# A gated long convolution: pitch of the x2 rows, and the order in which the gate copies leave PSUM

## The chip, the cores and the metric

The kernel runs on one core of one Trainium2 chip. The metric is the time of one execution on the device in microseconds; the median of several executions is compared.

## What is computed

Two layers follow each other. The first is a gated linear recurrence over time, the second multiplies three projections of its output, one of which has gone through a circular convolution of the full sequence length (written with Fourier transforms in the reference). There are 4 sequences of 6272 steps with 256 channels.

```
# first layer
f = lower_bound + (1 - lower_bound) * sigmoid(f_logit);  i = 1 - f
for t in range(S):                      # S = 6272
    h = f[:, t] * h + i[:, t] * x[:, t];  y[:, t] = h
# second layer, on y
x1, x2, x3 = split(y @ w_proj, 3)       # 256 channels each
x2_conv = irfft(rfft(x2, axis=1) * rfft(filter_fft, axis=0), axis=1)
out = (x1 * x2_conv * x3) @ w_out
```

## The kernel before

**Stages.** For each sequence b: `hgrn(b)` loads f_logit and x in 13 chunks of 512 steps, takes the sigmoid on ACT (line 303), multiplies on POOL (line 305, tile XT), transposes both on TensorE (line 312) and scans on DVE (line 334); the state is kept transposed in HA, in f16. `spectrum(b)` projects x2 (`phase_p`), makes the first transform step out of it (`phase_f1`, line 655, and `unit`'s line 700), multiplies by the filter's transform (line 713, DVE; line 705 fills one slot of each product on POOL) and transforms back (line 723, copied to Th at line 272). `gate(b)` makes x1 and x3 and their product z. `phase_o(b)` finishes the convolution (line 756), multiplies by z (line 762), projects (line 774), copies (line 274) and stores (line 784).

**Order.** All operations are entered in a plan with their readers and writers, and are then given out in the order that is written out in the string ORDER. It fixes for every operation the engine and the PSUM bank, so every engine has a fixed sequence in which the four sequences' stages are interleaved: hgrn of sequence b+1, spectrum, gate and output of sequence b run side by side. The costs written beside the operations take no part any more when the order is given. The change leaves ORDER as it is. Waits between engines are semaphores derived from the tiles that are read and written.

**The x2 rows.** A sequence of 6272 = 128 x 49 steps is laid out as 49 residues r (Q = 49) on the free side and 128 on the partitions. X2 holds for each of 128 pairs of channels one row of PW = 113 elements in f16: 49 residues of one channel at 0, a gap of 15 zeros at 49 to 63 (eight of them, tile Hm, later hold a part of the filter's transform), and 49 residues of the other channel at 64. `phase_p` fills it: for each group of four residues 8 matmuls (line 642) put 4 x 256 values in PSUM, and one copy (lines 272 and 277, by engine; profile name X<-PS) writes them to X2 as runs of four f16, one run for each channel, 256 runs in all. The thirteenth group has one residue, and writes 256 single elements. `phase_f1` reads 128 elements from the start of each row as the weights of a matmul, 15 elements into the next row when the pitch is 113. In the preparation X2 serves as a landing buffer for the filter (tags raw), and two memsets zero the gaps and the end (lines 571 and 574). The filter itself goes through a tile of the same layout in f32, f2, with the same pitch.

**The gate.** For each of 13 chunks of ten blocks of 49 steps (the last has eight), and each half of the channels, two matmul pairs (line 361) put x1 and x3, 490 values per partition in order of time, in PSUM. ACT copies each to SBUF (line 373, tiles x1s and x3s, f32, two buffers each, in turn), and POOL multiplies them (line 377) into zt, where the residue comes first and the block second: it writes runs of ten f16. Before the change the copies keep the order of time, and the product reads both tiles with steps of 49 elements.

Of the kernel before, what the change touches and what calls it, by code (L numbers as in the profile page):

```python
# [10 lines left out]
F32R = mybir.dt.float32r  # L11
F16 = mybir.dt.float16
I32 = mybir.dt.int32
AOP = mybir.AluOpType
AF = mybir.ActivationFunctionType
# [9 lines left out]
Q = 49  # L25
# [10 lines left out]
NEP = 128  # L36
# [3 lines left out]
HS = 64.0 / S  # L40
ZS = 64.0
OS = 1.0 / 4096.0
PW = 113
NX2 = 13
WR = 3072
AW = 4096
# [142 lines left out]
def kernel(  # L189
# [10 lines left out]
    nc = tc.nc  # L200
# [4 lines left out]
    op = plan.op  # L205

    konst = ctx.enter_context(tc.tile_pool(name="konst", bufs=1))
    iden = konst.tile([128, 128], F32, name="iden")
# [21 lines left out]

    X2 = konst.tile([128, NEP * PW + 16], F16, name="X2")
    xv = X2[:, 0:NEP * PW].rearrange("m (i c) -> m i c", c=PW)

# [10 lines left out]
    late = {}  # L244
# [4 lines left out]
    PS = psp.tile([128, 8, 512], F32, name="PS")  # L249
# [98 lines left out]
    def gate(b):  # L348
        for c in range(NCHK):
            m0 = c * XR  # L350
            nm = min(XR, 128 - m0)
            hn = [("hn", kh, i) for kh in range(2) for i in range(max(c - 1, 0), c + 1)]
            t0, n = m0 * Q, nm * Q
            for jb in range(2):
                x13 = []
                for i in range(2):
                    js = slice(i * 256 + jb * 128, i * 256 + jb * 128 + 128)

                    def mm(e, p, js=js, t0=t0, n=n):
                        for kh in range(2):  # L360
                            nc.tensor.matmul(PS[:, p, 0:n], W13[:, kh, js],  # L361
                                             HA[:, HB[kh] + t0:HB[kh] + t0 + n],
                                             start=(kh == 0), stop=(kh == 1))
                    x13.append(op("x13", {"PE": 0.005 + 2 * n / 2400.0}, mm,
                                  r=hn + ["W13"], w=["qX"], take=1))
                j = count["s"] % 2
                count["s"] += 1

                def xs(i, j=j, n=n):
                    return late["x3s" if i else "x1s"][:, j, 0:n]  # L370
                for i in range(2):
                    op("xs", {"ACT": 0.05 + n / 1200.0}, lambda e, p, xs=xs, n=n, i=i:
                       nc.scalar.activation(  # L373
                           xs(i), PS[:, p, 0:n], AF.Copy, scale=1.0 if i else ZS),
                       r=["cv"], w=[("x1s", j, i)], src=x13[i])
                op("z", {"POOL": 0.1 + 3.68 * n / 1000}, lambda e, xs=xs, jb=jb, m0=m0, nm=nm:
                   nc.gpsimd.tensor_tensor(  # L377
                       late["zt"][:, jb, :, m0:m0 + nm],
                       xs(0).rearrange("p (m r) -> p r m", r=Q),
                       xs(1).rearrange("p (m r) -> p r m", r=Q), op=AOP.mult),  # L380
                   r=[("x1s", j, 0), ("x1s", j, 1), "cv"], w=[("z", jb, c)])


    def prepare(tmp):
        dve, pool, act = nc.vector, nc.gpsimd, nc.scalar
# [13 lines left out]
        for i in range(2):  # L399
            small(lambda e, i=i: dve.tensor_copy(rot[:, i * 128:(i + 1) * 128], iden[:]), 128,  # L400
                  r=["iden"], w=["rot"], kind="turns")
# [16 lines left out]
        for kh in range(2):  # L418
# [4 lines left out]
               r=["om"] + Wr(1), w=["W13"])  # L423
            for p in range(2):
# [4 lines left out]
                   r=["om"] + Wr(1), w=["W2"])  # L429
# [5 lines left out]
        w = scr[:, 2016:4080].bitcast(F32)  # L435
# [24 lines left out]
        def args(e):  # L460
# [42 lines left out]
           w=["v", "sin"], table="sin")  # L503
# [30 lines left out]
        for i in range(WARM):  # L534
            op("warm", {"PE": 0.435}, warm, r=["iden"], take=1)

        f2 = tmp.tile([128, NEP * PW + 16], F32R, name="f2")

        def gaps(e):

            pool.tensor_copy(f2[:, 0:NEP * PW].rearrange("m (i c) -> m i c", c=PW)[:, :, Q:64],
                             iden[:, 0:15].unsqueeze(1).broadcast_to([128, NEP, 15]))
            pool.tensor_copy(f2[:, NEP * PW:], iden[:, 0:16])
        small(gaps, 1920, r=["iden"], w=["f2e"], e="POOL", kind="pad")
        afs = tmp.tile([128, 2, 2, UE, 64], F32R, name="afs")
        fv = f2[:, 0:NEP * PW].rearrange("m (g p c) -> m p g c", p=2, c=PW)
        ff = moe_filter_fft.rearrange("(a r) d -> a r d", r=Q)
        for g, r0 in enumerate(range(0, Q, 4)):
            rn = min(4, Q - r0)
# [21 lines left out]
        op("pad", {"POOL": 2.0}, lambda e: nc.gpsimd.memset(  # L571
            X2[:, 0:NEP * PW].rearrange("m (i c) -> m i c", c=PW)[:, :, Q:64], 0.0),
           w=[("raw", i) for i in range(7)] + [("x2", g) for g in range(NX2)] + ["Hm"])
        op("pad", {"POOL": 0.1}, lambda e: nc.gpsimd.memset(X2[:, NEP * PW:], 0.0),
           w=[("x2", 1)])
        mX = tmp.tile([128, 2, NEP], F32R, name="mX")
        for u in range(NU):
            af = afs[:, u % 2]
            for h in range(2):

                def first(e, pb, j=u * UE + h * 4):
                    pa = PS[:, pb:pb + 2].rearrange("m a (i c) -> m (a i) c", c=256)
                    for i in range(4):
                        nc.tensor.matmul(pa[:, i, :], f2[:, (j + i) * PW:(j + i) * PW + 128],  # L584
                                         D1r[:].rearrange("m x k -> m (x k)"), start=True, stop=True)
                f1 = op("FF1", {"PE": 0.475}, first,
                        r=[("f2", g, p) for g in range(13) for p in range(2)] + ["D1r", "f2e"],
                        w=[("FF1", u, h)], take=2)
                op("afs", either(512), lambda e, pb, af=af, h=h: copy(
                    e, af[:, :, 4 * h:4 * h + 4],  # L590
                    PS[:, pb:pb + 2].rearrange("p a (i x r k) -> p r (a i) x k", x=2, r=2, k=64)
                    [:, :, :, 0]), w=[("af", u % 2, h)], src=f1)
            small(lambda e, af=af, u=u: pool.tensor_copy(
                mX[:, :, u * UE:(u + 1) * UE], af[:, :, :, 0]), 100,
                r=[("af", u % 2, 0), ("af", u % 2, 1)],
                w=["mX"], e="POOL", kind="mX")

            def second(e, pb, af=af):
                for r in range(2):
                    for e2 in range(2):  # L600
                        rows = slice(64 * e2, 64 * e2 + 64)
                        nc.tensor.matmul(PS[:TB, pb + e2, :], FTr[rows, r, 0:TB], af[rows, r],  # L602
                                         start=(r == 0), stop=(r == 1))
            f2nd = op("FF2", {"PE": 0.45}, second,
                      r=[("af", u % 2, 0), ("af", u % 2, 1), "FTr"], w=[("FF2", u)], take=2)
            hw, ht = hws[u % len(hws)][0], [hws[u % len(hws)][1]]
            op("hw", either(1024), lambda e, pb, hw=hw: copy(e, hw[:TB], PS[:TB, pb:pb + 2], HS),
               w=ht, src=f2nd)
            for i, (p0, n) in enumerate(((0, TB), (TB, 64))):
                op("hst", {"SP": 0.36}, lambda e, hw=hw, u=u, p0=p0, n=n: nc.sync.dma_start(  # L610
                    H[u][p0:p0 + n], hw[0:n].rearrange("p e k -> p (e k)")),
                   r=ht, w=[("H", u, i)], dma=0.6 - 0.25 * i, lag=1.7)
# [233 lines left out]
```

## Time and profile before

| what | value |
|---|---|
| median of 3 runs | 494.39 us (493.84 to 494.9) |
| profiled execution | 494.1 us |
| its span, from the first to the last instruction | 492.3 us |
| granted TensorE clock | 0.998 |
| products of x1 and x3 on POOL (line 377) | 104, 201.5 us busy |
| copies of x1 and of x3 on ACT (line 373) | 208, 122.2 us busy |
| copies of x2 on DVE, on ACT (X<-PS) | 29 and 23, 41.6 and 33.9 us busy |
| POOL, busy in the span | 74% |

The profile is one execution, taken by the hardware profiler. A group of instructions is named by its source line, its engine, its operation, and its output and inputs; busy time is summed, and a mean duration of one is given in nanoseconds. Idle time of an engine is put down to whoever ended it. The chain is followed back from the last instruction, at each step to what released it. TensorE's matmuls overlap each other, so its busy time is not a measure of its use. Tile names are shortened where they end in digits: X is X2, f is f2, D is D1; HA also holds the first transform's output A.

### The profile page before, as it was taken

The numbers are of one execution on the slowest core, as the hardware profiler recorded it, in microseconds if no ns is written. First come the engines' busy times: TensorE is split into PE (matmuls) and PEld (weight loads), VectorE is DVE, ScalarE is ACT, GpSimd is POOL, SyncE is SP. The second block draws the span as 40 slices with busy tenths as digits, with TensorE's granted clock in tenths as the row PEclk, the third lists the DMA queues.
The fourth block names the chain that finished last, engine by engine and source line by source line (L and its number), as shares of the span: only waits on it lengthen the run. The fifth ranks groups of instructions, "written<-read, shape, count | busy, mean of one in ns | idle before, by whom it ended". The sixth has DMA issues, their size and how long they took to land.

```text
span 492.3 us, 13180 instructions
## 1 busy us (share of the span) xinstructions
PE 474.2 (96%) x5257; PEld 373.5 (76%) x5257; DVE 430.6 (87%) x449; ACT 427.7 (87%) x618; POOL 364.9 (74%) x299
## 2 busy tenths in 40 slices
PE   7999999999999999999999999999989999999894
PEld 6888788767768999677677888667778897666683
DVE  7678998799999998889989989899989988898773
ACT  5988899899999879899899888999888878999554
POOL 5587767899999425999999536999898443999700
PEclk9999999999999999999999999999999999999999
DMA  8979989575696899286857996467867861444166
GB/s 333 397 275 309 322 293 327 158 230 172 198 271 199 276 357 293 68 257 205 259 158 270 348 312 185 150 203 234 267 236 266 342 223 53 143 140 156 46 262 263
DMA packets 41725, 116.39 MB, mean 236 GB/s; under 512 B 4384, under 2 KB 6304, under 8 KB 41664
## 3 DMA queue, kind: packets, MB, share of 16 engines
q1 hardware_dynamic: 41664, 115.56, 69.9%
q8 instruction: 41, 0.67, 0.6%
q14 instruction: 20, 0.16, 0.1%
HBM read 84.54 MB, written 31.00 MB: 235 GB/s over the span
## 4 chain that ended last, share of the span: by engine, by line
PE 75%; ACT 7%; POOL 6%; DMA 5%; issue 3%; DVE 3%; SPq 0%; ACTq 0%; DVEq 0%; POOLq 0%
PE PS L312 15%; PE PS L361 13%; PE PS L642 9%; PE PS L774 8%; PE PS L723 7%; PE PS L700 5%; PE PS L655 5%; PE PS L756 5%; PE PS L584 3%; POOL zt L377 3%; DMA out_dram<-osb 2%; DVE PP L713 2%; PE PS L602 2%; ACT osb L274 2%; DMA FL<-in_f_logit_dram 2%
## 5 line engine op out<-in xcount | busy, mean ns | idle before, releaser
L377 POOL TENSOR_TENSOR zt<-x1s,x3s 128x490 f16<-128x490 f32 (+1 forms) x104 | 201.5, 1959 | 23.7 <-ACT x3s L373 16.2
L305 POOL TENSOR_TENSOR XT<-XT,FL 128x1024 f32<-128x1024 f32 (+1 forms) x52 | 117.3, 2258 | 58.7 <-ACT FL L303 41.1
L713 DVE TENSOR_TENSOR PP<-PS,Hu 98x1008 f16<-98x1008 f32 x128 | 147.4, 1199 | 11.3 <-ACT x3s L373 4.6
L334 DVE TENSOR_TENSOR_SCAN HA<-fTs,HA,PS 128x512 f16<-128x512 f32 (+1 forms) x96 | 113.9, 1203 | 5.2 <-PE PS L312 2.8
L361 PE MATMUL PS<-HA,W 128*128 128x490 f16 (+1 forms) x416 | 106.7, 368 | 1.4 <-ACT x3s L373 0.6
L762 DVE TENSOR_TENSOR ys<-PS,zt 128x1024 fp32r<-128x1024 f32 (+1 forms) x52 | 59.3, 1150 | 12.1 <-PE PS L756 7.3
L326 ACT ACTIVATE fTs<-PS,nomc 128x512 f32<-128x512 f32 (+1 forms) x87 | 59.2, 682 | 10.4 <-PE PS L312 8.3
L274 ACT ACTIVATE osb<-PS 128x1024 f32<-128x1024 f32 (+1 forms) x51 | 50.2, 990 | 19.7 <-PE PS L774 15.3
L373 ACT ACTIVATE x1s<-PS 128x490 f32<-128x490 f32 (+1 forms) x104 | 61.4, 594 | 5.5 <-PE PS L361 3.2
L373 ACT ACTIVATE x3s<-PS 128x490 f32<-128x490 f32 (+1 forms) x104 | 60.8, 590 | 5.5 <-PE PS L361 3.6
L312 PE MATMUL PS<-iden,XT 128*128 128x128 f32 x392 | 61.9, 278 | 0.7 <-POOL XT L305 0.3
L312 PE MATMUL PS<-iden,FL 128*128 128x128 f32 x392 | 61.0, 276 | 0.7 <-DVE X L277 0.7
L774 PE MATMUL PS<-Wo,ys 128*128 128x256 f32 x392 | 58.6, 293 | 1.0 <-DVE ys L762 0.8
L723 PEld LDWEIGHTS <-PP 98*128 98x128 f16 x1024 | 49.9, 98 | 11.9 <-issue 3.5
L272 ACT CAST Th<-PS 128x784 f16<-128x784 f32 x64 | 53.5, 836 | 2.6 <-PE PS L723 2.0
L303 ACT ACTIVATE FL<-FL 128x1024 f32<-128x1024 f32 (+1 forms) x52 | 53.0, 1022 | 1.5 <-DMA FL<-in_f_logit_dram 1.5
L361 PEld LDWEIGHTS <-W 128*128 128x128 f16 x416 | 35.1, 98 | 25.1 <-issue 7.4
L723 PE MATMUL PS<-VA,PP 98*128 98x98 f16 x512 | 52.2, 207 | 1.6 <-DVE PP L713 1.3
L774 PEld LDWEIGHTS PS<-Wo,ys 128*128 128x128 f32 x392 | 49.6, 189 | 4.8 <-DVE ys L762 1.8
L312 PEld LDWEIGHTS PS<-iden,XT 128*128 128x128 f32 x392 | 44.4, 140 | 10.9 <-issue 3.0
L723 PE MATMUL PS<-VB,PP 98*128 98x98 f16 x512 | 52.0, 207 | 0.0
L272 ACT CAST HA<-PS 128x1024 f16<-128x1024 f32 x49 | 50.3, 1032 | 1.6 <-PE PS L655 1.0
(105 smaller groups left out, 697.8 us busy)
## 6 DMA issues: line engine op xcount, KB each, us to landing
Hu<-H SPq DMA_DIRECT2D x64, 392.0 KB
FL<-in_f_logit_dram SPq DMA_DIRECT2D x48, 512.0 KB
XT<-in_x_dram SPq DMA_DIRECT2D x48, 512.0 KB
out_dram<-osb SPq DMA_DIRECT2D x48, 512.0 KB
X<-in_moe_filter_fft_dram SPq DMA_DIRECT2D x9, 512.0 KB
H<-Hu SPq DMA_DIRECT2D x16, 196.0 KB
H<-Hu SPq DMA_DIRECT2D x16, 128.0 KB
Hu<-in_moe_filter_fft_dram SPq DMA_DIRECT2D x2, 512.0 KB
```

What stands on the lines that cost most here:

```text
L272: nc.scalar.copy(dst, src)
L274: nc.scalar.activation(dst, src, AF.Copy, scale=scale)
L305: op("u", {"POOL": 0.1 + 0.553 * nb}, lambda e, xt=xt, ft=ft: nc.gpsimd.tensor_tensor(xt, xt, ft, op=AOP.mult), r=[("ft", k)], w=[("xt", k)])
L312: nc.tensor.transpose(PS[:, p, j:128 * nb:nb], src[:, j, cols], iden[:])
L334: nc.vector.tensor_tensor_scan(h, fT, PS[:, p, 0:n], init, op0=AOP.mult, op1=AOP.add),
L361: nc.tensor.matmul(PS[:, p, 0:n], W13[:, kh, js], HA[:, HB[kh] + t0:HB[kh] + t0 + n], start=(kh == 0), stop=(kh == 1))
L373: nc.scalar.activation(xs(i), PS[:, p, 0:n], AF.Copy, scale=1.0 if i else ZS),
L377: nc.gpsimd.tensor_tensor(late["zt"][:, jb, :, m0:m0 + nm], xs(0).rearrange("p (m r) -> p r m", r=Q), xs(1).rearrange("p (m r) -> p r m", ...
L713: nc.vector.tensor_tensor(PP[:TB, k, o, :, :, 1:64], px.unsqueeze(1).broadcast_to([TB, 2, UE, 63]), hh[:, :, :, 1:64], op=AOP.mult)
L723: nc.tensor.matmul(PS[:, ib + o, pr * TB:(pr + 1) * TB], PP[:TB, k, o, n, 2 * pr:2 * pr + 2, :], v[:TB], start=(n == 0), stop=(n == 1))
L762: nc.vector.tensor_tensor(late["ys"][:, yk, :, 0:rn * 128], PS[:, cb:cb + 2, 0:rn * 128], late["zt"][:].rearrange("p k r m -> p k (r m)") ...
L774: nc.tensor.matmul(po[:, i, :], late["ys"][:, yk, kh, i * 128:(i + 1) * 128], Wo[:, kh, :], start=(kh == 0), stop=(kh == 1))
```

## The change

The pitch of X2 becomes 116, while f2 keeps 113 under a name of its own (PF). The three elements at the end of each row, which the matmul weights of line 655 now read too, are zeroed by one more memset in the preparation. In the gate the copies on ACT read PSUM with the residue first and the block second, in steps of 49 elements, and write one run; the product then reads both tiles in one run. Its output, the number of instructions apart from the memset, and the order are the same.

```diff
-PW = 113
+PW = 116
+PF = 113
...
                 def xs(i, j=j, n=n):
-                    return late["x3s" if i else "x1s"][:, j, 0:n]
+                    return late["x3s" if i else "x1s"][:, j, 0:n].rearrange("p (r m) -> p r m", r=Q)
                 for i in range(2):
                     op("xs", {"ACT": 0.05 + n / 1200.0}, lambda e, p, xs=xs, n=n, i=i:
                        nc.scalar.activation(
-                           xs(i), PS[:, p, 0:n], AF.Copy, scale=1.0 if i else ZS),
+                           xs(i), PS[:, p, 0:n].rearrange("p (m r) -> p r m", r=Q), AF.Copy,
+                           scale=1.0 if i else ZS),
                        r=["cv"], w=[("x1s", j, i)], src=x13[i])
                 op("z", {"POOL": 0.1 + 3.68 * n / 1000}, lambda e, xs=xs, jb=jb, m0=m0, nm=nm:
                    nc.gpsimd.tensor_tensor(
                        late["zt"][:, jb, :, m0:m0 + nm],
-                       xs(0).rearrange("p (m r) -> p r m", r=Q),
-                       xs(1).rearrange("p (m r) -> p r m", r=Q), op=AOP.mult),
+                       xs(0), xs(1), op=AOP.mult),
...
-        f2 = tmp.tile([128, NEP * PW + 16], F32R, name="f2")
+        f2 = tmp.tile([128, NEP * PF + 16], F32R, name="f2")
...
-        op("pad", {"POOL": 0.1}, lambda e: nc.gpsimd.memset(X2[:, NEP * PW:], 0.0),
-           w=[("x2", 1)])
+
+        def tails(e):
+            nc.gpsimd.memset(xv[:, :, 113:PW], 0.0)
+            nc.gpsimd.memset(X2[:, NEP * PW:], 0.0)
+        op("pad", {"POOL": 0.6}, tails, w=[("raw", i) for i in range(7)] + [("x2", 1)])
...
-                        nc.tensor.matmul(pa[:, i, :], f2[:, (j + i) * PW:(j + i) * PW + 128],
+                        nc.tensor.matmul(pa[:, i, :], f2[:, (j + i) * PF:(j + i) * PF + 128],
```

More of the change, by code (lines that the diff above doesn't have):

```diff
@@ L535, in prepare @@
             op("warm", {"PE": 0.435}, warm, r=["iden"], take=1)
-        f2 = tmp.tile([128, NEP * PW + 16], F32R, name="f2")
+        f2 = tmp.tile([128, NEP * PF + 16], F32R, name="f2")
         def gaps(e):
-            pool.tensor_copy(f2[:, 0:NEP * PW].rearrange("m (i c) -> m i c", c=PW)[:, :, Q:64],
+            pool.tensor_copy(f2[:, 0:NEP * PF].rearrange("m (i c) -> m i c", c=PF)[:, :, Q:64],
                              iden[:, 0:15].unsqueeze(1).broadcast_to([128, NEP, 15]))
-            pool.tensor_copy(f2[:, NEP * PW:], iden[:, 0:16])
+            pool.tensor_copy(f2[:, NEP * PF:], iden[:, 0:16])
         small(gaps, 1920, r=["iden"], w=["f2e"], e="POOL", kind="pad")
         afs = tmp.tile([128, 2, 2, UE, 64], F32R, name="afs")
-        fv = f2[:, 0:NEP * PW].rearrange("m (g p c) -> m p g c", p=2, c=PW)
+        fv = f2[:, 0:NEP * PF].rearrange("m (g p c) -> m p g c", p=2, c=PF)
         ff = moe_filter_fft.rearrange("(a r) d -> a r d", r=Q)
```

## The prediction

> **What bounds the kernel now.** I read the page's busy times first, then the chain that ended last.
>
> ```profile
> span 492.3 us, 13180 instructions
> ...
> PE 474.2 (96%) x5257; PEld 373.5 (76%) x5257; DVE 430.6 (87%) x449; ACT 427.7 (87%) x618; POOL 364.9 (74%) x299
> ...
> PE 75%; ACT 7%; POOL 6%; DMA 5%; issue 3%; DVE 3%; SPq 0%; ACTq 0%; DVEq 0%; POOLq 0%
> PE PS L312 15%; PE PS L361 13%; PE PS L642 9%; PE PS L774 8%; PE PS L723 7%; PE PS L700 5%; PE PS L655 5%; PE PS L756 5%; PE PS L584 3%; POOL zt L377 3%; DMA out_dram<-osb 2%; DVE PP L713 2%; PE PS L602 2%; ACT osb L274 2%; DMA FL<-in_f_logit_dram 2%
> ```
>
> TensorE is the frame: three quarters of the chain are its matmuls. POOL holds 6% of the chain, half of it the products of line 377, which the change shortens. I therefore asked next how long anybody stands still for POOL, or for the x2 copies (tile X), in the waits:
>
> ```profile
> POOL zt L377 <- ACT x3s L373: 16.2, 13, 9.0
> ...
> PEld L723 <- POOL PP L705: 2.6, 6, 1.0
> ...
> ACT x3s L373 <- POOL zt L377: 1.2, 3, 0.6
> ...
> PEld PS L312 <- DVE X L277: 1.1, 1, 1.1
> ...
> PEld PS L312 <- POOL XT L305: 0.9, 3, 0.5
> ...
> PEld L655 <- DVE X L277: 0.7, 2, 0.4
> ...
> PE PS L642 <- ACT X L272: 0.6, 1, 0.6
> ```
>
> (Total us, times, longest.) The waits are short. POOL, in turn, waits 16.2 us for the copies that feed it. Last I read single costs, with shapes kept apart:
>
> ```profile
> L377 POOL TENSOR_TENSOR zt<-x1s,x3s 128x490 f16<-128x490 f32 x96 | 188.7, 1986 | 23.0 <-ACT x3s L373 15.5 <-DVE ys L762 6.2 <-ACT x1s L373 0.6
> ...
> L305 POOL TENSOR_TENSOR XT<-XT,FL 128x1024 f32<-128x1024 f32 x48 | 114.4, 2385 | 47.3 <-ACT FL L303 36.6 <-DMA XT<-in_x_dram 7.6 <-PE PS L312 1.9
> ...
> L373 ACT ACTIVATE x3s<-PS 128x490 f32<-128x490 f32 x96 | 56.6, 595 | 4.7 <-PE PS L361 2.8 <-POOL zt L377 1.2 <-ACT x1s L373 0.2
> L272 ACT CAST Th<-PS 128x784 f16<-128x784 f32 x64 | 53.5, 836 | 2.6 <-PE PS L723 2.0
> ...
> L274 ACT ACTIVATE osb<-PS 128x1024 f32<-128x1024 f32 x48 | 49.0, 1027 | 19.5 <-PE PS L774 15.3 <-PE PS L756 2.2 <-DMA out_dram<-osb 1.4
> ...
> L277 DVE CAST X<-PS 128x1024 f16<-128x1024 f32 x28 | 40.3, 1489 | 7.4 <-PE PS L642 7.3
> ...
> L272 ACT CAST X<-PS 128x1024 f16<-128x1024 f32 x20 | 29.9, 1518 | 3.7 <-PE PS L642 2.5 <-DVE X L277 0.9
> ...
> L272 ACT CAST X<-PS 128x256 f16<-128x256 f32 x3 | 4.0, 1350 | 0.9 <-PE PS L642 0.9
> ...
> L305 POOL TENSOR_TENSOR XT<-XT,FL 128x256 f32<-128x256 f32 x4 | 2.9, 733 | 11.4 <-DMA XT<-in_x_dram 4.7 <-ACT FL L303 4.5 <-ACT fTs L326 2.2
> ```
>
> **Part 1, the product z (104 on POOL).** Now both inputs are read 49 f32 apart and one costs 1986 ns; afterwards they are read in one run. The row for POOL products of two f32 inputs in one run is XT: from 733 ns at 256 elements to 2385 at 1024 it rises 2.151 ns per element, with 182 ns fixed. At 490 elements this is 1236 ns, at 392 it is 1025 (the eight small ones have 1634 now). The output stays as it was, runs of ten f16, which no XT row shows; if that is what costs, the product stays at 1986. I take 1236, because 4.03 ns per element against 2.33 in XT goes with the one thing that differs on the reading side, and the other reading is kept as a rival. POOL sheds 96 x 0.750 + 8 x 0.609 = 76.9 us of 364.9.
>
> What of it reaches the end? Bound from above: 3.1% of the chain is zt, 15.3 us; 750/1986 of it is 5.8 us. The order on every engine stays, so an end earlier than that would need other pieces of this chain to shrink. Bound from below: nothing, if at each place another path ends at once. The places can be looked at. Around 244 to 261 us the chain runs through six products on a POOL that hardly rests (16.98 of 17 us busy between 245 and 262), and then hands to TensorE; at 306 to 309 it goes product, copy, TensorE. The timeline there:
>
> ```profile
> 261.32 0.66 PE L312 MATMUL PS<-iden,XT 128*128 128x128 f32 x4 [0.29 <-POOL XT L305]
> ...
> 308.31 0.58 ACT L373 ACTIVATE x3s<-PS 128x490 f32<-128x490 f32 x1 [0.64 <-POOL zt L377]
> ...
> 308.94 0.57 PE L361 MATMUL PS<-HA,W 128*128 128x490 f16 x2 [0.59 <-ACT x3s L373]
> ```
>
> TensorE had been idle only 0.29 and 0.59 us there: POOL's path leads the others by no more than that, and a POOL that comes microseconds sooner wins just those tenths. So I add up what stands still for POOL: 2.6 (weights for I2, waiting for line 705, which queues behind z) + 0.9 (transposes waiting for XT, which queues behind z too) = 3.5 us. ACT's 1.8 us for a free x1s or x3s buffer (1.2 above and 0.6 for x1s) I leave out, as the ACT work queued behind waits for TensorE next. What is late next is then TensorE's own work, and on POOL the copies of line 373. Part 1: -3.5 us, between -5.8 and 0.
>
> **Part 2, the copies that read PSUM by strides of 49 (208 on ACT).** 595 ns now, one run to one run. Afterwards each reads ten elements 196 bytes apart, 49 times, and writes one run. The nearest row is Th: the same engine reads PSUM in fours 392 bytes apart. From 595 at 490 to 1027 at 1024 elements the one-run copies rise 0.809 ns per element, which gives 833 ns at 784; Th has 836. So strides are free there, and I take 0. From the other side: the x2 copies, with strides of 1024 bytes, have 1518 ns against 1027, 0.48 ns per element more; at 490 elements that is 235 ns, 49 us of ACT in all. But the x2 copy of 256 elements reads PSUM in one run and still has 1350 ns (a one-run osb copy of 256 has 397), so its price lies at its scattered writes, and Th is the nearer row. ACT cannot be faster than 595 here: nothing is taken from the work.
>
> [...]
>
> **Part 3, x2 rows 116 elements apart.** The copies write runs of four f16 (8 bytes). At 113 elements only every fourth row begins on a multiple of 8 bytes, at 116 all do. Th writes such aligned runs at full speed, so the ACT copies may go from 1518 to 1027 and the DVE copies from 1489 to 1214 (the DVE copies of 1024 f16 from PSUM into HA): 20 x 0.49 + 28 x 0.275 = 17.5 us of two engines; at the other end they stay. I take the fast end. The four copies of 256 elements write single f16 wherever they begin; between 397 and 1350 ns I take 1350, the row of the same operation. The phase itself does not get shorter: the chain in order of time has its 98 matmuls of line 642 in 10.85 us without a gap from 183.66 us on, and DVE waits for them (7.3 us in the X row). What counts is the ends of the phase: TensorE's 1.1 + 0.7 + 0.6 = 2.4 us in the waits above. The 1.1 (at 92 us) and the 0.6 (at 411 us) stand behind copies of 256 elements, so I leave them; the 0.7 are two waits behind copies that end 0.28 us sooner. Part 3: -0.6 us, between -2.4 and 0.
>
> [...] The trace has Th, runs of the same length, at 836 ns, and X at 1518; the row decides, and 0.6 us hangs on it.
>
> **Part 4, the extra memset** of 128 x 3 elements on POOL in the preparation: between the two fills of lines 571 (1920 elements, 1822 ns) and 574 (16 elements, 109 ns) 384 elements make 0.44 us. It comes at 66.2 us ahead of three wrap copies and one XT product; 6 us later POOL idles 1.72 us for FL. Cost 0 under that cover, 0.4 without. The 32 DVE products of line 677 read Hm 232 instead of 226 bytes apart; they take 10.8 us in all, so I take 0, and a tenth either way would be 1.1 us of DVE. DMAs, tables and the order of all queues stay.
>
> **Sum:** -3.5 - 0.6 = -4.1 us; the profiled execution took 494.1 us (span 492.3 and 1.8 around it), the median of the runs is 494.4. 494.4 - 4.1 = 490.3 us.
>
> **Rivals.**
> (a) The whole lead of the chain is paid out: -5.8 and -2.4, 486.2 us. For it: POOL is busy 20.00 of 20 us between 100 and 120 and between 420 and 440. Against it: the idle tenths at the places shown.
> (b) Hidden, or the product doesn't get cheaper, since its price is the writing: 493.7 to 494.4 us. For it: POOL's 16.2 us of waits for ACT, which a faster POOL only lengthens.
> (c) Slower: strided reads cost ACT. Its mechanism is part 2's upper side, its place the gate stage. The f2 copies on ACT (512 elements, strides of 1024 bytes) have 671 ns against 586 for the afs copies: 85 ns, 81 at 490 elements, 208 x 0.081 = 16.9 us. In eleven stretches of the gate stages (between 93 and 463 us, 242 us in sum) ACT is busy 223.1 us; this would fill it to 240. With half of it surfacing (an estimate: half of ACT's 18.9 idle us lie where it can be used) the time is 490.3 + 8.5 = 498.8; with 235 ns a copy, 515. It decides against the change from 40 ns a copy on (208 x 0.040 / 2 = 4.2, what the forecast wins). Against it: Th.
>
> **Chances.** A measurement of this kernel tells about 0.2%, 1 us, from no change. Forecast (488.4 to 493.4): 0.62; (a) 0.10; (b) 0.10; (c) 0.18. Faster is the forecast and (a), 0.72; same 0.10; slower 0.18. The range goes from (a)'s 486 to 495.5, which takes in (b) and the mild beginning of (c), and leaves out some 0.15. The forecast's own range is 488.4 to 493.4.
>
> **What would show it.** zt at 1.2 to 1.3 us and POOL near 290 us busy; x1s and x3s at 590 to 610 ns; X at 1.03 (ACT) and 1.21 (DVE), the small ones unchanged; PEld's waits for PP and XT mostly gone, POOL's wait for x3s much longer; the P phase still 10.9 us. Wrong would be: x1s above 635 ns, zt still near 2 us, or a fall of more than 8 us, which would mean that this chain was not the one that holds.

## The result, and the profile after

The changed kernel takes 494.03 us in the median of 20 executions (490.83 to 496.09), the kernel before took 493.88 in 20 of its own beside it (492.02 to 498.78). The ratio is 0.9994, with a 95% interval of 0.9975 to 1.0014: no difference. The forecast was 490.3. Each piece of work did become as short as it was meant to, and next to nothing of it reached the end.

The page of after begins with the span, the busy times and the shares of the chain that ended last:

```profile
span 492.1 us, 13181 instructions
...
PE 475.2 (97%) x5257; PEld 375.2 (76%) x5257; DVE 424.2 (86%) x449; ACT 419.0 (85%) x618; POOL 293.6 (60%) x300
...
PE 73%; DMA 9%; ACT 9%; DVE 4%; issue 3%; POOL 1%; SPq 0%; ACTq 0%; DVEq 0%; POOLq 0%
```

POOL went from 364.9 us busy to 293.6, and from 6% of the chain to 1%. The span went from 492.3 to 492.1. Lines after the change are numbered one to four higher than before: the gate's copies are line 374, its product 379, the copies 273, 275 (ACT) and 278 (DVE), the transposes 313, the x2 matmuls 646, I2 (the first step of the transform back, 723 before) 727, I1 (its second step, which finishes the convolution, 756 before) 760, the projection 778. The groups of after, with shapes kept apart (count, then busy time and mean ns of one, then idle time ahead of them):

```profile
L379 POOL TENSOR_TENSOR zt<-x1s,x3s 128x490 f16<-128x490 f32 x96 | 117.6, 1230 | 68.4 <-ACT x3s L374 48.5 <-ACT x1s L374 12.5 <-DVE ys L766 6.5
...
L374 ACT ACTIVATE x1s<-PS 128x490 f32<-128x490 f32 x96 | 57.5, 603 | 5.7 <-PE PS L362 3.6 <-issue 0.9 <-POOL HA L283 0.8
L374 ACT ACTIVATE x3s<-PS 128x490 f32<-128x490 f32 x96 | 56.9, 598 | 3.9 <-PE PS L362 3.1 <-ACT x1s L374 0.2
...
L278 DVE CAST X<-PS 128x1024 f16<-128x1024 f32 x28 | 33.9, 1229 | 12.4 <-PE PS L646 12.3
L273 ACT CAST X<-PS 128x1024 f16<-128x1024 f32 x20 | 20.7, 1048 | 9.4 <-PE PS L646 9.4
...
L273 ACT CAST X<-PS 128x256 f16<-128x256 f32 x3 | 4.0, 1325 | 1.9 <-PE PS L646 1.8
```

The product has 1230 ns (1986 before), the strided copies from PSUM 603 and 598 (595 for x3s before), the x2 copies 1229 on DVE (1489) and 1048 on ACT (1518). The last column tells what became of the shorter work: it became waiting. POOL's products wait 68.4 us (23.0 before), the x2 copies wait 12.3 and 9.4 us for TensorE's matmuls (7.3 and 2.5 before). The waits of after that answer to those of before (total us, times, longest):

```profile
POOL zt L379 <- ACT x3s L374: 50.2, 38, 10.7
...
PEld L727 <- POOL zt L379: 1.0, 1, 1.0
...
PEld PS L313 <- POOL XT L306: 0.3, 2, 0.2
...
PEld L727 <- POOL PP L709: 0.2, 1, 0.2
```

The weight loads wait for POOL 1.5 us now instead of 3.5, so 2.0 us of waits did go, without any time going. That is the first thing to explain. The second turned up on the way: the executions of one and the same kernel lie up to 7 us apart, and most of what could be won lies in that spread.

### The profile page after: what moved, and what is told of

The parts are those of the page before. It is cut to its first block, busy times and chain, and to the rows that moved or that the text cites. A ratio compares the mean times of both kernels' runs of the same rounds, so it can differ in the third digit from the quotient of the medians.

```text
span 492.1 us, 13181 instructions
## 1 busy us (share of the span) xinstructions
PE 475.2 (97%) x5257; PEld 375.2 (76%) x5257; DVE 424.2 (86%) x449; ACT 419.0 (85%) x618; POOL 293.6 (60%) x300
## 4 chain that ended last, share of the span: by engine, by line
PE 73%; DMA 9%; ACT 9%; DVE 4%; issue 3%; POOL 1%; SPq 0%; ACTq 0%; DVEq 0%; POOLq 0%
PE PS L313 15%; PE PS L362 15%; PE PS L646 9%; PE PS L727 7%; DMA out_dram<-osb 7%; PE PS L704 5%; PE PS L778 5%; PE PS L659 5%; PE PS L760 3%; PE PS L588 3%; ACT osb L275 3%; DVE PP L717 2%; PE PS L606 2%; DMA FL<-in_f_logit_dram 1%; DMA X<-in_moe_filter_fft_dram 1%
## 5 line engine op out<-in xcount | busy, mean ns | idle before, releaser
L379 POOL TENSOR_TENSOR zt<-x1s,x3s 128x490 f16<-128x490 f32 (+1 forms) x104 | 125.8, 1214 | 72.7 <-ACT x3s L374 50.2
L717 DVE TENSOR_TENSOR PP<-PS,Hu 98x1008 f16<-98x1008 f32 x128 | 147.4, 1200 | 10.2 <-ACT x3s L374 4.4
L327 ACT ACTIVATE fTs<-PS,nomc 128x512 f32<-128x512 f32 (+1 forms) x87 | 59.2, 683 | 10.2 <-PE PS L313 8.2
```

Source lines behind the costliest of these rows:

```text
L379: nc.gpsimd.tensor_tensor(late["zt"][:, jb, :, m0:m0 + nm], xs(0), xs(1), op=AOP.mult),
L717: nc.vector.tensor_tensor(PP[:TB, k, o, :, :, 1:64], px.unsqueeze(1).broadcast_to([TB, 2, UE, 63]), hh[:, :, :, 1:64], op=AOP.mult)
```

## The experiments

All ratios are against executions of the kernel before on the same chip, in turn with the kernel tried; n is the number of its executions.

**Half of the change each.** z_only is the kernel before with the strided copies and the product in one run; the pitch stays 113. x2_only is the kernel after with the old copies and the old product; the pitch stays 116. The edit of x2_only against after, cut to what matters:

```diff
-                    return late["x3s" if i else "x1s"][:, j, 0:n].rearrange("p (r m) -> p r m", r=Q)
+                    return late["x3s" if i else "x1s"][:, j, 0:n]
...
-                           xs(i), PS[:, p, 0:n].rearrange("p (m r) -> p r m", r=Q), AF.Copy,
-                           scale=1.0 if i else ZS),
+                           xs(i), PS[:, p, 0:n], AF.Copy, scale=1.0 if i else ZS),
...
-                       xs(0), xs(1), op=AOP.mult),
+                       xs(0).rearrange("p (m r) -> p r m", r=Q),
+                       xs(1).rearrange("p (m r) -> p r m", r=Q), op=AOP.mult),
```

> Only the gate copies and the product as in the change; x2 rows at 113. Theory A: matmuls 0.7 to 1.4 us ahead at 320 to 460 us, products 1230 ns, and the clock at half in the last output stage in part of the executions; time of the others near 492.8 us. Theory B: within 0.2 us of before all along.

> Only the x2 rows at 116; gate copies and product as before. Theory A (the gain exists, about 1.3 us by the start of the last output stage, most of it from the product, and is lost again when the granted clock falls to half for 3.4 us there): TensorE's matmuls run 0.3 to 0.6 us ahead of the kernel before from 200 us on, X copies 1229 and 1048 ns, time 493 to 494 us, executions with a mean clock under 0.996 about 1.5 us slower than the others. Theory B (nothing of the change reaches TensorE; the drift of the matmuls is noise): matmuls within 0.2 us of before all along.

z_only: 492.74 us (490.4 to 496.4, n 12), ratio 0.9989 (0.9962 to 1.0015). x2_only: 495.41 (490.95 to 497.91, n 12), ratio 1.0045 (1.002 to 1.0071). By itself the second would mean that the pitch costs 2 us. Of what was expected of the two traces neither theory came true. Lined up matmul by matmul with the trace of before, z_only leads by 1.3 us at 320 us and by 2.1 at 460, and x2_only is behind by 0.9 and 0.6; but before_again (below), the same program, leads by 0.3 at 460, and before_shift (below), which has nothing of the change, by 2.0. A lead in one trace says little. x2_only ran once more later, under the name x2_warm; in spite of the name it has no fill (told of below).

> The kernel with only the x2 rows at 116, once more and without the filling matmuls, to see whether its 0.45% over before in the first set is real. Theory A: it was chance, since all its instructions are as short or shorter: within 0.5 us of before. Rival E (the wider rows cost something outside the copies, a DMA or a wait): again 1.5 us or more above before.

It gave 494.95 us (491.27 to 497.01, n 12), ratio 0.9998 (0.9971 to 1.0025). The same program gave 1.0045 and 0.9998, on two chips, and the interval of the first leaves out the second. Sets of twelve carry more than their own interval says, so a difference of 0.4% in one set is not to be believed alone.

**The kernel before against itself.** It ran as a kernel of its own, with nothing edited.

> The kernel before, to see its granted clock in many executions. Theory A: most executions have a mean clock of 0.996 or more, fewer falls than the 11 of 20 of the changed kernel, and those that have one are about 1.5 us slower. Rival C: falls are as frequent as in the changed kernel and the two medians differ by nothing for another reason.

Median 494.5 (491.61 to 495.99, n 12), ratio 1.0011 (0.9988 to 1.0034). Its trace, with those of the later runs, settles a point of the prediction. The start at 308.94 us, where the forecast's timeline shows TensorE idle for 0.59 us behind a product of line 377 and a copy, is there without that wait in this second execution of the same program: its matmuls come 0.74 us sooner from there on, with the product as long as ever. Of all eighteen traces three have that wait: before, pair_shift_before and shift_only (0.59 to 0.75 us), and shift_only has the short product. So the wait goes with the execution and not with the length of the product.

The wait of 0.29 us at 261.32 (transposes behind XT) is there in all eight traces with the old product, at 0.3 us, and in none of the ten with the new one. Lined up with before, the ten gain 0.5 us there and lose half of it at the next transposes. At 270 us each of them has 0.25 to 0.27 us more lead than at 258; the seven others with the old product have changed by 0.05 at most. This is the one gain of the change that every trace shows. What follows it differs by more than that from one execution to the next.

**The clock of TensorE in the last output stage.** In the trace of after the granted clock is at half from 463.24 to 466.65 us, 3.41 us long; in that of before it is not, but in before_again it is (464.26 to 467.67). TensorE has two gaps of 0.9 us there, one ahead of the last I2, which waits for DVE's products, and one ahead of the first I1, which waits for Th. The changes of the recorded clock lie on a step in both traces: from 5.85 us to 463.24, from 463.24 to 466.65 and from 466.65 to 487.13 in after are 134, 1 and 6 times 3.413 us (457.386, 3.413 and 20.480 us), and from 5.72 to 490.42 in before is 142 times that (484.693 us). Stretches of this length, counted from the changes that each trace records, are called windows here; that the clock is decided from one window to the next is how the author reads them. In after, and then in before, two windows following each other (us, busy time of each engine with its instructions, granted clock, DMA share, GB/s):

```profile
459.83:463.24 3.41, 1.59 (x35) 1.32 (x33) 1.39 (x2) 2.42 (x5) 1.99 (x2) 1.00 0.02 5
463.24:466.65 3.41, 3.41 (x65) 3.21 (x61) 2.36 (x2) 0.00 (x0) 0.00 (x0) 0.50 0.00 0
```

```profile
459.70:463.11 3.41, 2.47 (x39) 1.69 (x34) 2.81 (x3) 3.12 (x6) 3.41 (x4) 1.00 0.02 5
463.11:466.52 3.41, 2.46 (x75) 2.14 (x71) 1.37 (x2) 0.81 (x1) 1.50 (x1) 1.00 0.00 0
```

In after one window holds both gaps, TensorE is busy 1.6 of its 3.41 us, and the next window has half the clock. In before the edge falls between the gaps, each window has one, TensorE is busy 2.5 us in each, and the clock stays. Of the ten traces without the fill in which the windows were laid out, five have one window with 1.59 to 1.95 us (after, before_again, x2_only, shift_only, pair_shift_after), and all five fall; five have two with 2.47 (before, x2_warm, z_only, before_shift, pair_shift_before), and none falls. By these ten the bound lies between 1.95 and 2.47 us of 3.41. Windows laid out in the same way through all 18 traces narrow it to about 2 us, and busy time alone doesn't sort those next to it: one of 2.05 us (after, 483.72 to 487.13) is followed by half clock, one of 2.01 us (pair_fill_before, 292.66 to 296.07) is not; with 1.95 or less every window is, with 2.12 or more none. Which of the two happened near 463 us went with where the edge lay: at 463.11 us in before, between the gaps, and at 464.26 in before_again, the same program, with both gaps in the 3.41 us ahead of it (TensorE busy 1.58 us). The kernel called warm fills the place: after, with ten matmuls more that nobody reads, five ahead of the last I2 and five ahead of the first I1 of the last sequence.

```diff
+    def busy(p, n):
+        for i in range(n):
+            nc.tensor.matmul(PS[:, p, 0:392], D1[:], W13[:, 0, 0:392], start=True, stop=True)
...
+            if b == 3 and u == 15:
+                busy(ib, 5)
...
+                if b == 3 and g == 0:
+                    busy(cb, 5)
```

> The changed kernel with ten extra matmuls that fill TensorE's idle time just before the last output stage (five ahead of the last I2, five ahead of the first I1 of the last sequence; their results are overwritten). Theory A: the clock stays full up to the end of the matmuls in nearly every execution (mean 0.996 or more), the 64 matmuls of line 760 at the start of that stage take 2.0 us, not 3.5, and the median is 492.5 to 493.0. Rival C (the give-back comes from waiting for stores, not from the clock): the median stays at 494.

Median 491.8 us (490.83 to 492.63, n 12), ratio 0.9971 (0.9955 to 0.9987). In the timeline of TensorE (start, length, then what), the first I1 block in after and in warm:

```profile
463.13 3.53 PE L760 MATMUL PS<-ID,Th 64*128 64x128 f16 x64 [0.90 <-ACT Th L273]
```

```profile
463.30 1.98 PE L768 MATMUL PS<-ID,Th 64*128 64x128 f16 x64
465.32 2.34 PE L786 MATMUL PS<-Wo,ys 128*128 128x256 f32 x16
```

64 matmuls take 1.98 us instead of 3.53. None of the eight traces with the fill falls there. What a fall costs can be read from the traces: lined up with before, the five that fall lose 1.3 to 1.5 us between 463 and 470 us, and the twelve others lose nothing (0.02 us or less).

Over the executions without a trace there is only the mean clock, and it is a rough sign. It also counts the half clock behind the last matmul (in after from 487.13 us on, the last matmul ending at 486.54), which costs nothing, and two of the five traces that fall have a mean of 0.996 (before_again, x2_only). A mean under 0.995 comes in 38 of 115 executions without the fill (the executions of before that were run for comparison left out) and in 1 of 76 with it; that one, the profiled execution of pair_fill_before, has its half clock in the preparation, at 9.36 to 12.77 us. fill_only (below) is not among the 76: it has 6 of 12. By this sign a fall is worth about what the traces say: in shift_only (below) the runs at 0.995 or more have a mean of 491.5 us, the others of 492.7; in pair_shift_after it is 490.4 and 492.3.

**The fill without the change, and with half of it.** before_warm is before with the ten matmuls, z_warm is z_only with them.

> The kernel before with the ten filling matmuls. Theory A (the falling clock costs both kernels about the same 1.5 to 2 us; what the change itself brings is small): 491.5 to 492.3 us, spread as small as in the changed kernel with them (491.8 us, 490.8 to 492.6). Rival D (the change brings 1.5 to 2 us and loses it by more frequent falls of the clock): 493 us or more.

> Only the gate copies and the product, with the ten filling matmuls. Theory A: within 0.5 us of the kernel before with them. Rival E: 1 us or more faster than the whole change with them (491.8).

before_warm: 492.42 us (490.37 to 493.99, n 12), ratio 0.9948 (0.9922 to 0.9973). z_warm: 492.02 (490.85 to 493.97, n 12), ratio 0.9946 (0.9922 to 0.997). The fill is worth as much without the change, and the fast product adds nothing that could be told from chance (means 492.17 against 492.40).

**POOL almost freed.** If what is left of the gate's product sets the end anywhere, taking it away must show. z_small_warm is after with the fill, and its product covers one of 49 residues in sequences 1 to 3; the rest of z is left out there.

```diff
-                        late["zt"][:, jb, :, m0:m0 + nm],
-                        xs(0), xs(1), op=AOP.mult),
+                        late["zt"][:, jb, 0:q, m0:m0 + nm],            # q = Q if b == 0 else 1
+                        xs(0)[:, 0:q], xs(1)[:, 0:q], op=AOP.mult),
```

> The changed kernel with the filling matmuls, and in the sequences 1 to 3 the product covers one residue of 49 only, so that POOL has next to nothing to do for it. Theory A (POOL is off the path, whatever it does): within 0.5 us of 491.8. Theory F (POOL's queue still holds TensorE, so that part 1 was only half paid): 1.5 us or more faster.

Median 492.06 us (489.55 to 495.06, n 12), ratio 0.9954 (0.9925 to 0.9983). Its page and waits:

```profile
PE 474.6 (97%) x5267; PEld 374.2 (76%) x5267; DVE 424.0 (86%) x449; ACT 419.3 (86%) x618; POOL 216.4 (44%) x300
...
PE 82%; ACT 6%; DMA 4%; DVE 4%; issue 2%; POOL 1%; SPq 0%; ACTq 0%; DVEq 0%; POOLq 0%
```

```profile
POOL zt L379 <- ACT x3s L374: 85.8, 45, 16.8
```

The products of the three sequences, by form:

```profile
L379 POOL TENSOR_TENSOR zt<-x1s,x3s 128x10 f16<-128x10 f32 x72 | 14.9, 209 | 93.9 <-ACT x3s L374 75.2 <-ACT x1s L374 17.0 <-PE PS L733 1.4
```

POOL is busy 216.4 us, 148 less than before and 77 less than in after, and the mean is 492.27 against 492.40 on the same chip for before_warm, whose POOL does everything in the old way (the difference has a standard error of 0.5). 77 us more of freed POOL time end up in POOL's wait for x3s (50.2 to 85.8 us) and in other waits of POOL. So the length of the product isn't what sets the end, to within about 1 us; POOL's 6% of the chain in before was, by that, one of several ways through the graph that were nearly equally long.

**What the fill did besides.** In warm, TensorE's lead over after, lined up matmul by matmul, grew a second time, by 0.9 us (from 1.3 to 2.2), between 469 and 475 us, where its clock was full in both. The copies osb on ACT (tile of the stores, three buffers in turn) in after, then in warm:

```profile
467.86 1.97 ACT L275 ACTIVATE osb<-PS 128x1024 f32<-128x1024 f32 x2 [4.79 <-PE PS L778]
470.73 1.02 ACT L275 ACTIVATE osb<-PS 128x1024 f32<-128x1024 f32 x1 [0.91 <-PE PS L778]
473.52 1.02 ACT L275 ACTIVATE osb<-PS 128x1024 f32<-128x1024 f32 x1 [1.76 <-DMA out_dram<-osb]
```

```profile
466.56 2.16 ACT L275 ACTIVATE osb<-PS 128x1024 f32<-128x1024 f32 x2 [3.31 <-PE PS L786]
469.44 1.03 ACT L275 ACTIVATE osb<-PS 128x1024 f32<-128x1024 f32 x1 [0.72 <-PE PS L786]
471.19 2.12 ACT L275 ACTIVATE osb<-PS 128x1024 f32<-128x1024 f32 x2 [0.72 <-PE PS L786]
```

The fourth copy of after waits 1.76 us until the first store has landed and its buffer is free; that of warm waits for TensorE only. One packet of 16 KB on the queue q8 (instruction) differs. In after it begins at 470.37 us, after the first store's first packet (469.76); in warm at 467.41, ahead of it (468.47). The DMA view of one microsecond of each, 470 to 471 us of after and 467 to 468 of warm (packets, MB, share of 16 engines):

```profile
q8 instruction: 1, 0.02, 6.5%
```

```profile
q8 instruction: 1, 0.02, 8.7%
```

How this reaches the copy can be read from the small packets of the store's own queue. In these traces a store of 512 KB ends with 16 packets of 4 bytes. In after 15 of those of the first store begin at 471.04 to 471.20 us and the sixteenth only at 472.92, behind 15 of the second store (472.34 to 472.50); 0.60 us later the fourth copy begins. In warm the sixteenth begins at 470.52. The packet counts of after (471 to 472 us, 472 to 473) and of warm (469 to 470, 470 to 471), where the packets under 512 B are these:

```profile
DMA packets 110, 0.39 MB, mean 389 GB/s; under 512 B 15, under 2 KB 15, under 8 KB 110
DMA packets 73, 0.23 MB, mean 234 GB/s; under 512 B 16, under 2 KB 16, under 8 KB 73
```

```profile
DMA packets 100, 0.35 MB, mean 348 GB/s; under 512 B 15, under 2 KB 15, under 8 KB 100
DMA packets 99, 0.40 MB, mean 401 GB/s; under 512 B 1, under 2 KB 1, under 8 KB 99
```

So fifteen of the sixteen packets that end the first store come in time and one is late. The instruction packet, 1.04 us long in after and begun in the midst of that store, fits as what holds the one up; that both go over the same one of the 16 DMA engines is not in the trace.

The fill put 20 instructions (matmuls and weight loads) ahead, and the packet came 2.96 us sooner (467.41 against 470.37 us), the first store 1.29 us (468.47 against 469.76); that the one moved the other is the author's estimate from these times. Two kernels part the two effects. shift_only is after with ten more of the small matmuls that run during the preparation, and no fill; fill_only is warm with ten fewer of them, so that its instruction stream stands at the stage as in after.

```diff
-        def warm(e, p):
+        def warm(e, p, n=4):
...
-            for i in range(4):
+            for i in range(n):
...
         for i in range(WARM):                  # the first ten groups of 32: n = 5 (shift_only), 3 (fill_only)
```

> The kernel after, with ten more of the small matmuls with which TensorE is kept busy during the preparation (ten of the 32 groups have 5 instead of 4), and none in the last output stage. It moves TensorE's instruction stream by the same 20 instructions as the fill did, and fills no idle time there. Theory F (the fill gained twice: some 1.5 us because TensorE kept its full clock, some 1.3 us because the 16 KB instruction packet came ahead of the first store of the last stage): the packet comes ahead of the first store, the fourth osb copy does not wait for a store, and the median is 1.3 us under that of after, near 492.7; half clock still appears in some executions near 464 us. Theory G (the clock alone): the median is that of after, 494.0 within 0.7, whichever comes first.

> The kernel with the fill (after, ten filling matmuls around the start of the last output stage), but ten matmuls fewer in the preparation, so that TensorE's instruction stream stands at that stage as it does in after. Theory F: no half clock, but the instruction packet meets the first store again, the fourth osb copy waits 1 to 2 us for it, and the median is 1.3 us above that of the filled kernel, near 493.1. Theory G: 491.8 as with the fill, within 0.7.

shift_only: 492.3 us (490.26 to 493.45, n 12), ratio 0.9948 (0.9929 to 0.9966). fill_only: 493.28 (490.45 to 495.26, n 12), ratio 0.9978 (0.9954 to 1.0002). Again the copies osb, of shift_only and of fill_only:

```profile
468.17 1.97 ACT L275 ACTIVATE osb<-PS 128x1024 f32<-128x1024 f32 x2 [4.78 <-PE PS L778]
471.05 1.03 ACT L275 ACTIVATE osb<-PS 128x1024 f32<-128x1024 f32 x1 [0.91 <-PE PS L778]
472.79 1.98 ACT L275 ACTIVATE osb<-PS 128x1024 f32<-128x1024 f32 x2 [0.72 <-PE PS L778]
```

```profile
465.82 2.17 ACT L275 ACTIVATE osb<-PS 128x1024 f32<-128x1024 f32 x2 [3.32 <-PE PS L786]
468.70 1.03 ACT L275 ACTIVATE osb<-PS 128x1024 f32<-128x1024 f32 x1 [0.72 <-PE PS L786]
471.52 1.02 ACT L275 ACTIVATE osb<-PS 128x1024 f32<-128x1024 f32 x1 [1.80 <-DMA out_dram<-osb]
```

shift_only has the half clock (463.65 to 467.06 us) and no wait of the fourth copy; fill_only has the full clock and the wait. The packet begins at 467.78 us in shift_only, ahead of the first store's first packet at 470.07, and at 467.98 in fill_only, after 467.73. So both effects are there, each without the other, as theory F said. Over the 18 traces: in all seven where the instruction packet begins after the first store's first packet ACT idles 1.4 to 2.2 us ahead of the fourth copy, which begins 0.57 to 0.60 us after the store's last small packet (in before and before_again too, where the profile puts the wait down to a matmul of line 756); in ten of the eleven where it begins ahead the copy waits for TensorE alone, 0.7 us, and in one (pair_shift_before) for a store, 0.77 us. The six programs that were traced twice have it on the same side both times. That fill_only's median is the 493.1 that was expected is partly luck: six of its twelve executions have a mean clock under 0.995, which the fill was to prevent. Where it fell in them no trace shows; in its profiled execution it did not. The preparation is one place where it may: with ten matmuls fewer, TensorE is busy 2.12 us in windows between 4.7 and 10.2 us of that trace, close above the bound, and pair_fill_before falls there after a window of 1.57 us.

**The stores.** half_stores_warm is after with the fill, storing 128 of the 256 columns of the result; the other half is left out.

```diff
-                out[b].rearrange("(a r) d -> a r d", r=Q)[:, r0:r0 + rn, :],
-                late["osb"][k][:, 0:rn, :]),
+                out[b].rearrange("(a r) d -> a r d", r=Q)[:, r0:r0 + rn, 0:128],
+                late["osb"][k][:, 0:rn, 0:128]),
```

> The kernel after with the fill, storing only 128 of the 256 columns of the result (the other half is left out, the number of stores and their issues stay). Theory C (what is left of the spread and of POOL's lost gain sits in waits for stores): osb's waits for out_dram fall under 0.5 us, the last store lands 1 us or more sooner, and the median is 489 to 490.5. Theory H (stores are beside the path but for the last one): 491.3 to 491.8 with waits gone but TensorE no sooner at 460 us.

Median 488.7 us (487.85 to 490.24, n 6), ratio 0.9883 (0.9855 to 0.991): 3.1 us under warm. But TensorE came no sooner: against the trace of before its matmuls lead by 0.91 us at 460 and by 2.15 at the end, in warm by 1.11 and 2.35. What is saved lies behind the last matmul, in the landing of the last stores: from the end of the last matmul to the end of the span are 3.8 us, 5.6 in warm. That is 1.8 of the 3.1 us; the two ran on unlike chips, and the rest stays open. osb's waits for stores fell to 1.1 us, not under 0.5. Theory C comes near in the number and is wrong in the place; the bytes of the stores are beside TensorE's path until the end, as theory H said, whose time was 2.6 us too high.

**The change, with both disturbances out of the way.** before_shift is before with the ten matmuls in the preparation.

> The kernel before, with the same ten more small matmuls in the preparation as in shift_only, and nothing of the change. Theory F (the place of the instruction packet in the last output stage is worth 1.3 to 2 us and has nothing to do with the change): the packet comes ahead of the first store, and the median is 1.3 to 2.3 us under that of before, near 492.3, as in shift_only. Theory A (the change is worth 1 us or more once the packet is out of the way): at least 1 us above shift_only's 0.9948 of before, a ratio of 0.997 or more.

492.85 us (490.95 to 494.46, n 12), ratio 0.9984 (0.9965 to 1.0003). By the bound set ahead, 0.997, this speaks for the change being worth 1 us; but it ran on another chip than shift_only, and the pair with the fill (0.9971 with the change, 0.9948 without), on two chips as well, said the opposite. So both pairs were run once more, on one chip and beside the same 32 executions of before.

> shift_only again, on the same chip and beside the same runs of before as its partner without the change. Theory F (the change is worth nothing, the moved packet some 1 to 2 us): ratio within 0.0015 of its partner's. Theory A (the change is worth 1 us or more once the packet is out of the way): 0.002 or more under its partner.

> before_shift again, partner of pair_shift_after. Theory F: 0.9955 to 0.9975 of before. Theory A: 0.998.

> The kernel after with the fill, again, on the same chip as its partner without the change. Theory F: ratio within 0.0015 of its partner's, and both near 0.995 to 0.997. Theory A: 0.002 or more under its partner.

> The kernel before with the fill, again, partner of pair_fill_after. Theory F: 0.995 to 0.997 of before. Theory A: 0.997 to 0.998, with its partner at 0.995.

| disturbance removed by | with the change | without it | mean with, less mean without |
|---|---|---|---|
| moved packet | 0.9940 (0.9919 to 0.9962), 491.33 us, n 12 | 0.9952 (0.9932 to 0.9972), 491.48 us, n 11 | -0.44 us |
| fill | 0.9952 (0.9932 to 0.9971), 491.76 us, n 10 | 0.9969 (0.9948 to 0.9989), 492.14 us, n 12 | -0.58 us |

The partners differ by 0.0012 and 0.0017, about the 0.0015 of theory F and under the 0.002 of theory A. Each difference has a standard error of about 0.5 us; together the two are -0.5 us with one of 0.3, so the executions alone don't tell the change from nothing. The earlier pairs can't help, since their partners ran on unlike chips: taken each against before on its own chip, they differ by +0.3 us (fill) and -1.6 (packet). The change is worth about what the traces show at 261 us, some 0.3 us, perhaps as much as 1; it isn't worth the 4.1 that were forecast. More can't be told from these runs.

Moving the packet by ten matmuls that do nothing gave -0.5, -0.6, -0.2 and -0.5% in four sets, with and without the change. After with those ten matmuls has 0.9948 and 0.9940 of before.

## Why the prediction was wrong

**The durations (parts 1 to 3) were right.** 1230 ns for the product against 1236 from the XT row, 1026 against 1025 for the small ones, POOL 293.6 us busy against the "near 290" of the prediction; 598 and 603 ns for the strided copies against 590 to 610; 1048 and 1229 for the x2 copies against 1027 and 1214, the small ones unchanged. In part 4 the memset took 718 ns against 440, and cost nothing.

**The step that failed is the sum in part 1:** "So I add up what stands still for POOL: 2.6 (weights for I2, waiting for line 705, which queues behind z) + 0.9 (transposes waiting for XT, which queues behind z too) = 3.5 us." Both are rows of PEld, the weight loads. In after these rows are down to 1.5 us, and the time did not follow: a load that starts later was not yet a matmul that started later. TensorE's own rows stood in the same view of before (total us, times, longest):

```profile
PE PS L723 <- DVE PP L713: 1.3, 2, 0.9
...
PE PS L312 <- POOL XT L305: 0.3, 1, 0.3
```

In before the matmuls of I2 wait for DVE's products of line 713 and never for POOL; behind the preparation POOL holds a matmul up once, for 0.3 us at 261.32. By this row part 1 would have been 0.3 us instead of 3.5, and the forecast 493.5 with part 3 or 494.1 without. The ten traces with the short product show it at that size, 0.25 to 0.27 us. The upper bound of 5.8 us (the chain's 3.1% for zt) was a true bound, and a useless one: z_small_warm took the product down to 209 ns a piece in three sequences of four and gained nothing that could be told. The rival that came true is (b), hidden work, to which the prediction gave 0.10; what it named as evidence, POOL's 16.2 us of waits for ACT that a faster POOL only lengthens, is what happened (50.2 us).

**The second fault: two joins read from one execution.** The 0.59 us at 308.94 and the 0.29 at 261.32 were the ground for "a POOL that comes microseconds sooner wins just those tenths". They add up to 0.9 us, and the sum went on with the 3.5 of the weight loads instead; nor are both of them sure. The second execution of the same program doesn't have the 0.59, and shift_only has a wait of 0.75 there with the short product. The 0.29 us at 261.32 recur, and that step holds there: the gain is a few tenths.

**Part 3** was right in its reasoning, that the phase doesn't get shorter because TensorE sets it (DVE's wait for it went from 7.3 to 12.3 us), and its 0.6 us lie below what the runs can tell: 1.0045 and 0.9998 for the same program. **Part 2** was right; rival (c), strided reads that cost ACT, is excluded by 598 against 595 ns. The rival of the other end, (a), fell with part 1.

**What the prediction had no term for** is that the end of the kernel is decided by things beside the work that was shortened: whether the clock falls at the last stage (1.3 to 1.5 us in the traces), which changes from one execution to the next, and whether an instruction packet meets the first stores (0.5 to 1.3 us in the traces between 467 and 476), which goes with the program. Each is larger than the gain that the traces show for the change. What the packet's move is worth over the whole kernel, 2 us by the medians, is more than the 0.8 us that the trace of shift_only shows against after at that place (from 0.30 us behind to 0.54 ahead of it); whether the other 40 packets of that queue moved too, and what they contribute, was not followed.

## What to carry to other kernels

Price a shorter piece of work by the waits of the engine that sets the end itself, its matmul rows and not its weight loads, and profile the unchanged kernel a second time: a wait that isn't in both executions is no gain to count on. Before making an engine faster, let its work be done on a fraction of the data; a run of that kind shows the largest gain that can be had. Where executions of one kernel lie 1% apart, look for what differs between two traces of the same program, since it may be worth more than the change.

## What was not expected of the hardware

- TensorE's clock fell to half for 3.41 us after windows in which it had still been busy for 1.59 to 1.95 us, in gaps of no more than 0.92 us, and kept its full rate where the same two gaps fell into two windows (2.47 us busy in each). By the 18 traces the bound lies between 1.95 and 2.12 us of 3.41.
- One instruction packet of 16 KB, begun within the first of 6.4 MB of stores in the last output stage, goes with a store whose last of 16 closing packets begins 1.7 us after the others (in after), and the fourth copy into a ring of three buffers begins after 1.4 to 2.2 us of idle time instead of 0.7. With twenty instructions more on TensorE, at the stage or 400 us ahead of it, it began 1.06 us (warm) and 2.29 us (shift_only) ahead of that store.
- ACT reads PSUM in steps of 196 bytes at the price of one run (598 against 595 ns for 490 values). 256 runs of four f16 cost 1518 ns on ACT and 1489 on DVE when three rows of four begin off a multiple of 8 bytes from the tile's start (226 bytes apart), 1048 and 1229 when all begin on one (232 bytes apart), while 256 single f16 stayed at 1325 ns (ACT) and 1278 (DVE).
